# Score banks in a four-unit pattern and paired VectorE transposes in the backward core of a linear-attention plus multi-query-attention kernel

## The chip, the core and the metric

The kernel runs on one core of one Trainium2 chip. The metric is the device time of one execution in microseconds (us): the median of three executions before the change is 1065.62 us (1065.28 to 1067.54). The TensorE clock that was granted over the whole profiled execution is 0.999 of full speed. A unit of time used below is the "block" of eight units of the main loop, explained in the section on the kernel.

## The reference

The reference takes two attention layers, their inputs, weights and the gradient of the joint output, and returns the output and all nine gradients. Layer A is linear attention (feature map phi on q and k, no softmax). Layer B is softmax attention with 16 query heads and one shared key and value head. Cut to layer B, on which the change works:

```python
q = (x @ wq).reshape(B, S, H, Dh).transpose(0, 2, 1, 3)     # S = 2048, H = 16, Dh = 28
k, v = x @ wk, x @ wv                                        # one head for all
scores = jnp.einsum("bhqd,bkd->bhqk", q, k) * (Dh ** -0.5)
o = jnp.einsum("bhqk,bkd->bhqd", softmax(scores), v)
out_B = o.transpose(0, 2, 1, 3).reshape(B, S, H * Dh) @ wo
# returned: out = concat(out_A, out_B) and the vjp of it for x, wq, wk, wv, wo (and A's inputs)
```

For the gradients the kernel needs, per head, e = exp(scale * q k^T - shift) (not normalised), dP = dO v^T, dS = e * dP, and from them o = e v, dq = dS k, dk = dS^T q, dv = e^T dO. Normalisation and the row sums are folded into the small operands (a column of ones in v, the first column of dO).

## The kernel before

**Before the main loop** (up to about 218 us of the span) stand layer A with its gradients and the projections of layer B. **After it** (from about 1017 us) stand the last sums: dwq, dwk, dwv, dx of layer B and their stores.

**The main loop** (`for u in range(NU + 28)`, NU = 512) is a software pipeline written out by hand: inside `tc.manual_schedule()` every engine executes its instructions in the order in which the Python loop issues them. A block b = u // 8 is a pair of heads and 256 queries; unit u of it covers 256 of the 2048 keys for both heads h = 0, 1. Scores, dP and dS are kept transposed, keys on the 128 partitions: a tile 128 x 512 holds two groups of 128 keys by 256 queries. In iteration u the engines do:

- **TensorE**: `rows_SD(u)` makes the scores of unit u (banks `sp[0]`, `sp[1]` of PSUM, one per head) and dP of unit w = u - 16 (banks `DB[0]`, `DB[1]`, one buffer each). A product of 32 rows by 256 columns fills half a bank, so each bank takes two matmuls, and the list `todo` is their order. Then, in even iterations, the transposes `onat_T` (u % 8 = 2) and `don_T` (u % 8 = 6) and the output projection `out_proj` (u % 8 = 0), all three into the bank `spare`; then `o_dq`, which adds two units to o and two to dq (16 matmuls); then `dv_mm` (four matmuls a call, four calls a block). In odd iterations come 16 matmuls of dk (`dk_m`).
- **ScalarE**: exp of the first head's scores (line 924, "exp0"), the copy of `DB[1]` to SBUF (938, "cp"), exp of the second head's scores (970, "exp1"). Nothing else in the steady loop.
- **VectorE**: the product dS = dP * e of the first head, straight from `DB[0]` (936, "the product"); small evictions: `out_proj` (727) at u % 8 = 0, oTs (952) at 1, reciprocal and normalisation (799, 800) at 2, dq (955) at 3, a row sum (812) at 4, doT (828) at 6; and at the end of each iteration the 32 x 32 transpose of dS of unit y = u - 18 (1003, "the transpose", 512 words of two bf16 each), which dk reads.
- **GpSimd**: the product dS of the second head (939), small products, copies of queries, a few stores.
- **SyncE**: every four units one DMA transpose of e (972) into `eN`, which dv reads; four DMA transposes of queries every 64 units.

PSUM: three score banks `SB`, used round robin: iteration u takes `SB[2u % 3]` and `SB[(2u + 1) % 3]`, and the third is `spare`. So what is `spare` in an even iteration is the first score bank of the odd one that follows. Buffers in SBUF: `dsT` (dS) 5, one unit each; `eN` (transposed e) 6, four units each; `dsx` (transposed dS) 2, eight units each. `dsT` buffers are also used for staging outside the loop (`sbuf`).

Engines meet through semaphores, and a waiting instruction holds up what is behind it on its engine.

Of the kernel before, what the change touches and what calls it, by code (L numbers as in the profile page):

```python
# [16 lines left out]
D = 448  # L17
# [8 lines left out]
def kernel(  # L26
# [604 lines left out]
    with ExitStack() as cs_:  # L631
        pe_ = cs_.enter_context(tc.tile_pool(name="ceT", bufs=1, side="right"))
        pn_ = cs_.enter_context(tc.tile_pool(name="ceN", bufs=1, side="right"))
        pd_ = cs_.enter_context(tc.tile_pool(name="cdsT", bufs=5, side="right"))
# [10 lines left out]
        dsT, dsx, qX, don, doT, rl, prod = ({} for _ in range(7))  # L645
        ETs = [pe_.tile([P, 4, 2, 512], BF16, name=f"eT{i}") for i in range(5)]
        ENs = [pn_.tile([P, 32, P], BF16, name=f"eN{i}") for i in range(6)]
# [3 lines left out]

        def eN(b, c):
            return ENs[(2 * b + c // 2) % 6][:, 16 * (c % 2):16 * (c % 2) + 16, :]
# [9 lines left out]
        def rows_SD(u, sp, dp):  # L663
# [4 lines left out]
            if sp is not None and dp is not None and u % 2 == 0:  # L668
                todo = [(0, 0), (0, 1), (1, 0)] * 2 + [(1, 1)] * 2
# [71 lines left out]
        def post_load(k):  # L741
            if k == 4:
                post["dkvT"], mix = (eN(61, c).rearrange("p a b -> p (a b)") for c in range(2))
                post["dkvn"] = mix[:, 0:1024]
# [20 lines left out]
        def gwo(n0, n1):  # L765
            for n in range(n0, n1):
                st, g_ = (n // 2, n % 2) if n < 32 else (n % 16, n // 16)
                if st == 0:
                    post[g_] = SB[g_ % 2]
                al = post[g_]  # L770
                mm(al[:, 0:D], do_nat[:, st, g_ * P:(g_ + 1) * P], post["gb"][st][:, 0:D], start=(st == 0),
                   stop=(st == NS - 1))
                if st == NS - 1:
                    sb = pd_.tile([P, 2, 512], BF16, name="dsT")[:, 0, 0:D]
                    nc.scalar.activation(out=sb, in_=al[:, 0:D], func=ACT.Copy)
                    for j in range(4):
                        h = 4 * g_ + j
                        nc.gpsimd.dma_start(out_8[h * DH:(h + 1) * DH, :], sb[32 * j + 1:32 * j + 1 + DH, :])  # L778
# [116 lines left out]
        with tc.manual_schedule():  # L895
            nc.sync.dma_start(wo, wo_d[:, 0:D].rearrange("(g p) c -> p g c", p=P))
            qX[0] = pqa_.tile([P, 4, 2, 512], BF16, name="qX")
            for g in range(4):
                st = pd_.tile([P, 2, 512], BF16, name="dsT").rearrange("p a (n j) -> p a n j", j=32).rearrange(
# [4 lines left out]
            for u in range(NU + 28):  # L904
# [3 lines left out]
                sp = [SB[(2 * u + h) % 3] for h in range(2)] if hasS else None  # L908
                dp = DB if hasD else None
                spare = SB[(2 * u + 2) % 3] if hasS else SB[2]  # L910
                rows_SD(u, sp, dp)
                if (b := due(u, 10)) is not None:
                    onat_T(b, spare)
# [11 lines left out]
                if u == 1:  # L925
                    q_shift(pn3, shifts[3], [pd_.tile([P, 2, 512], BF16, name="dsT").rearrange("p a b -> p (a b)").bitcast(F32)
                                             for _ in range(1)])
# [4 lines left out]
                if hasD:  # L932
                    dst = pd_.tile([P, 2, 512], BF16, name="dsT")
# [35 lines left out]
                if hasS:  # L969
                    nc.scalar.activation(out=eT(u)[:, 1, :], in_=sp[1][:, :], func=ACT.Exp, scale=scale)  # L970
                    if u % 4 == 3:
                        nc.sync.dma_start_transpose(ENs[u // 4 % 6][:, :, :],
# [9 lines left out]
                else:  # L982
                    o_dq((u - 2, u - 1), (u - 20, u - 19))
                    b, n = divmod(u - 20, 8)
                    for k in {0: (0, 1), 2: (2,), 6: (3,)}.get(n, ()) if 0 <= b < NB else ():
                        dv_mm(dv_acc, b, k // 2, k % 2)
# [12 lines left out]
                if 0 <= y < NU:  # L999
                    b, tp = divmod(y, 8)  # L1000
                    if tp == 0:
                        dsx[b] = px_.tile([P, 8, 2, 2, 256], BF16, name="dsx")
                    nc.vector.transpose(  # L1003
                        out=dsx[b][:, tp, :, :, :].rearrange("p h t c -> p (h t c)").bitcast(F32),
                        in_=dsT[y][:, :, :].rearrange("p h c -> p (h c)").bitcast(F32))
# [11 lines left out]
        def sbuf():  # L1017
            return pd_.tile([P, 2, 512], BF16, name="dsT")[:, 0, :]
# [11 lines left out]
        def dwq(c):  # L1030
# [9 lines left out]
            if c == 3:  # L1040
                odd = pd_.tile([P, 2, 512], BF16, name="dsT").rearrange("p a b -> p (a b)").bitcast(F32)[0:64, 0:D]
# [77 lines left out]
```

## Time and profile before

| what | value |
|---|---|
| median of three executions | 1065.62 us |
| span of the profiled execution, first to last instruction | 1064.7 us |
| busy share of the span: TensorE, VectorE, ScalarE, GpSimd | 96%, 84%, 82%, 73% |
| first exp0 of the main loop starts at | 218.5 us |
| exp0 of unit 511 starts at | 989.0 us |
| last transpose ends about | 1017.6 us |
| mean time of eight units, from unit 24 to unit 504 | 12.11 us |

The profiled execution has a span of 1064.7 us. What lies around it in the measured time is about 0.9 us, if it stands at the median.

How to read the profile: "x512" is a count, then comes the busy time of the group and the mean length of one instruction. In the timeline a row is start, length, engine, line, operation, written tile <- read tiles; neighbours of one group are merged into one row (x2, x16). Both ScalarE and VectorE start an instruction before the end of the one ahead of it is recorded, so lengths overlap: the cost of an instruction on its engine is the distance between starts.

### The profile page before, as it was taken

Reading aid. Unit: us, or ns where it says so; the run is one execution under the profiler, and the core shown is the slowest. Engines: PE = TensorE matmul, PEld = TensorE weight load, DVE = VectorE, ACT = ScalarE, POOL = GpSimd, SP = SyncE. Lnnn points to the kernel's source line nnn. Section 1 sums busy time; section 2 is a strip of 40 time slices with the busy share of each in tenths; the row PEclk is TensorE's granted clock in tenths of the full one; section 3 lists DMA queues with packets and bytes.
Section 4 is the critical chain, followed back from the end, with each engine's and each line's share of the span. In section 5 each row is a group of like instructions: output and inputs, shape, how many; then the busy total and the mean of one; then the engine's idle time right before and its main releaser. Section 6 shows DMA issues by size and latency. Waiting matters only on the chain.

```text
span 1064.7 us, 40036 instructions
## 1 busy us (share of the span) xinstructions
PE 1023.1 (96%) x16241; PEld 489.1 (46%) x16241; DVE 899.5 (84%) x1797; ACT 870.4 (82%) x1741; POOL 780.7 (73%) x1033
## 2 busy tenths in 40 slices
PE   9999999998999999999999999999999999999998
PEld 5555455434444444444444444444444444444444
DVE  7887400459999999999999999999999999999942
ACT  6463222489999999999999999999999999999522
POOL 6001242218888898899889989988998999888881
PEclk9999999999999999999999999999999999999999
DMA  9849899079999999999999999999999999999963
GB/s 264 167 108 192 171 203 246 22 137 181 193 188 196 182 203 189 188 202 191 197 181 197 181 196 195 193 189 194 196 197 192 199 190 183 208 190 177 222 141 89
DMA packets 689937, 195.15 MB, mean 183 GB/s; under 512 B 670616, under 2 KB 687792, under 8 KB 689752
## 3 DMA queue, kind: packets, MB, share of 16 engines
q1 hardware_dynamic: 680152, 179.92, 99.6%
q0 software_dynamic: 4640, 8.71, 2.9%
q10 hardware_dynamic: 4960, 3.96, 1.3%
q8 instruction: 127, 2.08, 0.8%
q14 instruction: 58, 0.48, 0.2%
HBM read 12.60 MB, written 10.84 MB: 22 GB/s over the span
## 4 chain that ended last, share of the span: by engine, by line
PE 43%; ACT 32%; issue 14%; POOL 5%; DVE 4%; DMA 1%; ACTq 0%; DVEq 0%; POOLq 0%
ACT cp L938 16%; PE agen L81 14%; ACT eT L970 13%; PE agen L656 10%; PE aacc L656 10%; PE aacc L81 5%; POOL dsT L939 3%; PE aacc L790 2%; ACT eT L924 2%; PE aacc L821 1%; DVE dsT L936 1%; DVE dsx L1003 1%; DMA out_dram<-dsT 1%; POOL eT L754 1%; POOL out_dram L778 0%
## 5 line engine op out<-in xcount | busy, mean ns | idle before, releaser
L939 POOL TENSOR_TENSOR dsT<-cp,eT 128x512 bf16<-128x512 bf16 x512 | 587.9, 1156 | 78.9 <-ACT cp L938 71.7
L1003 DVE STREAM_TRANSPOSE dsx<-dsT 128x512 f32<-128x512 f32 x512 | 357.6, 699 | 2.9 <-POOL dsT L939 0.8
L656 PEld LDWEIGHTS <-R 32*128 32x128 bf16 (+1 forms) x9104 | 227.9, 94 | 274.1 <-issue 238.4
L936 DVE TENSOR_TENSOR dsT<-agen,eT 128x512 bf16<-128x512 f32 x512 | 341.7, 667 | 10.9 <-PE agen L656 5.6
L938 ACT ACTIVATE cp<-agen 128x512 bf16<-128x512 f32 x512 | 315.8, 617 | 12.3 <-PE agen L656 11.2
L924 ACT ACTIVATE eT<-aacc 128x512 bf16<-128x512 f32 x512 | 313.6, 612 | 14.8 <-PE agen L656 4.8
L970 ACT ACTIVATE eT<-aacc 128x512 bf16<-128x512 f32 x512 | 322.2, 629 | 0.0
L656 PE MATMUL agen<-dsx,qX 32*32 32x512 bf16 x4096 | 267.6, 375 | 0.0
L656 PE MATMUL agen<-doT,R 32*128 32x256 bf16 x2048 | 247.1, 269 | 3.4 <-DVE dsT L936 1.4
L656 PE MATMUL aacc<-R,R 32*128 32x256 bf16 (+1 forms) x2240 | 218.2, 268 | 7.2 <-DVE oTs L800 2.5
L656 PE MATMUL agen<-eT,R 128*32 128x256 bf16 x2048 | 157.5, 274 | 0.1
L656 PE MATMUL agen<-dsT,R 128*32 128x256 bf16 x2048 | 156.8, 274 | 0.1
L656 PEld LDWEIGHTS <-qX 32*32 32x32 bf16 x4096 | 79.8, 89 | 113.7 <-issue 53.3
L656 PE MATMUL aacc<-eN,don 128*32 128x512 bf16 x1024 | 97.1, 379 | 0.1
L81 PEld LDWEIGHTS <-R 128*128 128x128 bf16 (+1 forms) x517 | 40.8, 98 | 43.5 <-issue 11.5
L406 POOL COPY pk<-R 128x256 bf16<-128x256 bf16 x4 | 1.6, 397 | 73.8 <-DVE R L366 73.7
L81 PE MATMUL agen<-R,R 128*128 128x448 bf16 (+1 forms) x180 | 42.1, 361 | 0.6 <-ACT R L225 0.6
L832 POOL COPY qst<-R 128x512 bf16<-128x512 bf16 x56 | 34.2, 611 | 4.0 <-DMA qX<-qst 3.9
L656 PEld LDWEIGHTS <-don 128*32 128x32 bf16 x1024 | 33.8, 97 | 1.4 <-issue 1.0
L804 POOL TENSOR_TENSOR prod<-R,oTs 128x128 f32<-128x128 bf16 x64 | 27.6, 431 | 9.3 <-DVE oTs L800 9.3
L422 DVE TENSOR_TENSOR osb<-aacc,pr 64x448 bf16<-64x448 f32 x2 | 1.2, 618 | 38.3 <-DMA out_dram<-osb 24.4
L955 DVE TENSOR_SCALAR R<-agen 64x256 bf16<-64x256 f32 x64 | 27.3, 427 | 3.6 <-PE agen L656 1.6
(231 smaller groups left out, 967.8 us busy)
## 6 DMA issues: line engine op xcount, KB each, us to landing
out_dram<-osb ACTq DMA_DIRECT2D x22, 112.0 KB
eN<-eT SPq DMA_TRANSPOSE x128
xa<-in_A_x_dram SPq DMA_DIRECT2D x8, 224.0 KB
ga<-in_grad_out_dram SPq DMA_DIRECT2D x4, 448.0 KB
xa<-in_grad_out_dram POOLq DMA_DIRECT2D x4, 448.0 KB, 6.1
out_dram<-wdq POOLq DMA_DIRECT2D x8, 224.0 KB, 4.0
eT<-in_grad_out_dram SPq DMA_DIRECT2D x4, 448.0 KB
eT<-in_B_x_dram SPq DMA_DIRECT2D x4, 448.0 KB
```

The lines of the kernel that those rows point to most:

```text
L81: nc.tensor.matmul(out_ap, lhsT=lhsT, rhs=rhs, start=start, stop=stop, tile_position=(0, 0))
L656: nc.tensor.matmul(out, lhsT=lhsT, rhs=rhs, start=start, stop=stop, tile_position=pos, skip_group_check=True)
L790: nc.tensor.transpose(onp[:, qb, :, :].rearrange("p h c -> p (h c)"), oTs[0:64, qb * P:(qb + 1) * P], identF[0:64, 0:64], tile_position=(0 ...
L804: nc.gpsimd.tensor_tensor(out=prod[b][:], in0=dnv, in1=os_, op=ALU.mult)
L832: eng.tensor_copy(out=st.rearrange("p (b s) a j -> p b s a j", s=2)[:, :, s, :, :], in_=src.unsqueeze(2).to_broadcast([P, 4, 4, 32]))
L924: nc.scalar.activation(out=eT(u)[:, 0, :], in_=sp[0][:, :], func=ACT.Exp, scale=scale)
L936: nc.vector.tensor_tensor(out=dst[:, 0, :], in0=dp[0][:, :], in1=ew[:, 0, :], op=ALU.mult)
L938: nc.scalar.activation(out=cp[:, :], in_=dp[1][:, :], func=ACT.Copy)
L939: nc.gpsimd.tensor_tensor(out=dst[:, 1, :], in0=cp[:, :], in1=ew[:, 1, :], op=ALU.mult)
L955: nc.vector.tensor_scalar(out=qT_B[g][64 * hp:64 * hp + 64, qc * 256:(qc + 1) * 256], in0=oq[64:128, 0:256], scalar1=scale, scalar2=None, ...
L970: nc.scalar.activation(out=eT(u)[:, 1, :], in_=sp[1][:, :], func=ACT.Exp, scale=scale)
L1003: nc.vector.transpose(out=dsx[b][:, tp, :, :, :].rearrange("p h t c -> p (h t c)").bitcast(F32), in_=dsT[y][:, :, :].rearrange("p h c -> p ...
```

## The change

Four things are changed in the main loop, and two buffer sets are sized anew.

1. **Score banks.** The round robin over three banks is replaced by a pattern over four units: (first head, second head, spare) = (0, 1, 2), (0, 2, 1), (1, 0, 2), (1, 2, 0) for u % 4 = 0 to 3. In even iterations the spare bank is always bank 2, and it is the second head's bank of the odd iteration that follows; the first head of an odd iteration takes the same bank as the first head of the even one before.
2. **Order of the matmuls.** In odd iterations `todo` becomes first heads first: scores h0, dP h0, scores h0, dP h0, then scores h1, dP h1, scores h1, dP h1. Half of `o_dq` (o of unit u - 2, dq of unit u - 20) is issued directly after `rows_SD`, ahead of the transposes and of `out_proj`; the other half stays behind them.
3. **Transposes of dS.** dS of two units lies in one buffer (4 buffers of two units instead of 5 of one). One transpose of 1024 words at the end of each odd iteration replaces two of 512 words.
4. **dv.** The four calls of `dv_mm` of block b move from units 20, 20, 22, 26 to 18, 20, 20, 22 behind the block's first unit, and `eN` has 5 buffers instead of 6.

Staging tiles outside the loop now come from `half()`, which hands out the halves of a two-unit `dsT` buffer.

```diff
-        pd_ = cs_.enter_context(tc.tile_pool(name="cdsT", bufs=5, side="right"))
+        pd_ = cs_.enter_context(tc.tile_pool(name="cdsT", bufs=4, side="right"))
...
-        ENs = [pn_.tile([P, 32, P], BF16, name=f"eN{i}") for i in range(6)]
+        ENs = [pn_.tile([P, 32, P], BF16, name=f"eN{i}") for i in range(5)]
...
+        halves = []
+
+        def half():
+            if not halves:
+                t = pd_.tile([P, 2, 2, 512], BF16, name="dsT")
+                halves.extend([t[:, 0, :, :], t[:, 1, :, :]])
+            return halves.pop(0)
...
-            return ENs[(2 * b + c // 2) % 6][:, 16 * (c % 2):16 * (c % 2) + 16, :]
+            return ENs[(2 * b + c // 2) % 5][:, 16 * (c % 2):16 * (c % 2) + 16, :]
...
-            if sp is not None and dp is not None and u % 2 == 0:
-                todo = [(0, 0), (0, 1), (1, 0)] * 2 + [(1, 1)] * 2
+            if sp is not None and dp is not None:
+                todo = [(0, 0), (1, 0)] * 2 + [(0, 1), (1, 1)] * 2 if u % 2 else \
+                    [(0, 0), (0, 1), (1, 0)] * 2 + [(1, 1)] * 2
...
-                sp = [SB[(2 * u + h) % 3] for h in range(2)] if hasS else None
+                b0, b1, spare = ((SB[i] for i in ((0, 1, 2), (0, 2, 1), (1, 0, 2), (1, 2, 0))[u % 4]) if hasS else SB)
+                sp = [b0, b1] if hasS else None
                 dp = DB if hasD else None
-                spare = SB[(2 * u + 2) % 3] if hasS else SB[2]
                 rows_SD(u, sp, dp)
+                if u % 2 == 0:
+                    o_dq((u - 2,), (u - 20,))
...
-                    dst = pd_.tile([P, 2, 512], BF16, name="dsT")
+                    if w % 2 == 0:
+                        pairs[w // 2] = pd_.tile([P, 2, 2, 512], BF16, name="dsT")
+                    dst = pairs[w // 2][:, w % 2, :, :]
...
-                        nc.sync.dma_start_transpose(ENs[u // 4 % 6][:, :, :],
+                        nc.sync.dma_start_transpose(ENs[u // 4 % 5][:, :, :],
...
-                    o_dq((u - 2, u - 1), (u - 20, u - 19))
-                    b, n = divmod(u - 20, 8)
-                    for k in {0: (0, 1), 2: (2,), 6: (3,)}.get(n, ()) if 0 <= b < NB else ():
+                    o_dq((u - 1,), (u - 19,))
+                    b, n = divmod(u - 18, 8)
+                    for k in {0: (0,), 2: (1, 2), 4: (3,)}.get(n, ()) if 0 <= b < NB else ():
                         dv_mm(dv_acc, b, k // 2, k % 2)
...
-                if 0 <= y < NU:
+                if 0 <= y < NU and y % 2:
                     b, tp = divmod(y, 8)
-                    if tp == 0:
+                    if tp == 1:
                         dsx[b] = px_.tile([P, 8, 2, 2, 256], BF16, name="dsx")
                     nc.vector.transpose(
-                        out=dsx[b][:, tp, :, :, :].rearrange("p h t c -> p (h t c)").bitcast(F32),
-                        in_=dsT[y][:, :, :].rearrange("p h c -> p (h c)").bitcast(F32))
+                        out=dsx[b][:, tp - 1:tp + 1, :, :, :].rearrange("p u h t c -> p (u h t c)").bitcast(F32),
+                        in_=pairs[y // 2].rearrange("p u h c -> p (u h c)").bitcast(F32))
...
         def sbuf():
-            return pd_.tile([P, 2, 512], BF16, name="dsT")[:, 0, :]
+            return half()[:, 0, :]
```

More of the change, by code (lines that the diff above doesn't have):

```diff
@@ L643 @@
         oq, dk_acc = (psA.tile([P, 512], F32, name="agen") for _ in range(2))
-        dsT, dsx, qX, don, doT, rl, prod = ({} for _ in range(7))
+        dsT, dsx, qX, don, doT, rl, prod, pairs = ({} for _ in range(8))
         ETs = [pe_.tile([P, 4, 2, 512], BF16, name=f"eT{i}") for i in range(5)]
-        ENs = [pn_.tile([P, 32, P], BF16, name=f"eN{i}") for i in range(6)]
+        ENs = [pn_.tile([P, 32, P], BF16, name=f"eN{i}") for i in range(5)]
         def eT(u):
             return ETs[u // 4 % 5][:, u % 4, :, :]
+        halves = []
[4 more added lines that the diff above has]
+            return halves.pop(0)
         def eN(b, c):
-            return ENs[(2 * b + c // 2) % 6][:, 16 * (c % 2):16 * (c % 2) + 16, :]
+            return ENs[(2 * b + c // 2) % 5][:, 16 * (c % 2):16 * (c % 2) + 16, :]
         def mmt(out, lhsT, rhs, pos, start, stop):
@@ L742, in post_load @@
             if k == 4:
-                post["dkvT"], mix = (eN(61, c).rearrange("p a b -> p (a b)") for c in range(2))
+                post["dkvT"], mix = (eN(61, c).rearrange("p a b -> p (a b)") for c in (2, 3))
                 post["dkvn"] = mix[:, 0:1024]
@@ L773, in gwo @@
                 if st == NS - 1:
-                    sb = pd_.tile([P, 2, 512], BF16, name="dsT")[:, 0, 0:D]
+                    sb = half()[:, 0, 0:D]
                     nc.scalar.activation(out=sb, in_=al[:, 0:D], func=ACT.Copy)
@@ L898 @@
             for g in range(4):
-                st = pd_.tile([P, 2, 512], BF16, name="dsT").rearrange("p a (n j) -> p a n j", j=32).rearrange(
+                st = half().rearrange("p a (n j) -> p a n j", j=32).rearrange(
                     "p a (n b) j -> p (a n) b j", b=4)
@@ L925 @@
                 if u == 1:
-                    q_shift(pn3, shifts[3], [pd_.tile([P, 2, 512], BF16, name="dsT").rearrange("p a b -> p (a b)").bitcast(F32)
-                                             for _ in range(1)])
+                    q_shift(pn3, shifts[3], [half().rearrange("p a b -> p (a b)").bitcast(F32)])
+                    halves.clear()
                     dv_acc = psA.tile([P, 512], F32, name="aacc")
@@ L1040, in dwq @@
             if c == 3:
-                odd = pd_.tile([P, 2, 512], BF16, name="dsT").rearrange("p a b -> p (a b)").bitcast(F32)[0:64, 0:D]
+                odd = half().rearrange("p a b -> p (a b)").bitcast(F32)[0:64, 0:D]
                 nc.scalar.activation(out=odd, in_=al[64:128, 0:D], func=ACT.Copy)
```

## The prediction

> **What bounds the kernel now.** I looked first at the busy time by engine in a stretch of the main loop, then at the groups of VectorE in it, then at the timeline of single units, and last at the chain of work behind the loop. The stretch from 300 to 940 us (columns: length, then PE, weight loads, DVE, ACT, POOL busy with counts, clock, DMA share, GB/s):
>
> ```profile
> 300.00:940.00 640.00, 618.08 (x12141) 290.49 (x12138) 625.68 (x1216) 633.31 (x1274) 579.12 (x698) 1.00 1.19 193
> ```
>
> Three engines look full. Lengths overlap, however, so I go by distances between starts. ScalarE around an odd unit (559.54 starts exp0 of a unit with u % 8 = 3):
>
> ```profile
> 557.86 0.63 ACT L924 ACTIVATE eT<-aacc 128x512 bf16<-128x512 f32 x1
> 558.33 0.64 ACT L938 ACTIVATE cp<-agen 128x512 bf16<-128x512 f32 x1
> 558.81 0.66 ACT L970 ACTIVATE eT<-aacc 128x512 bf16<-128x512 f32 x1
> 559.54 0.60 ACT L924 ACTIVATE eT<-aacc 128x512 bf16<-128x512 f32 x1
> 560.03 0.59 ACT L938 ACTIVATE cp<-agen 128x512 bf16<-128x512 f32 x1
> ```
>
> The reader should see a step of 0.48 us from instruction to instruction, and 0.73 from exp1 of the even unit to exp0 of the odd one. Eight units at 24 x 0.48 are 11.5 us; they take 12.11 on average (11.97 to 12.02 in quiet blocks). The 0.6 us are lost before odd exp0s alone (means 0.57, 0.76, 0.59, 0.57 in place of 0.48), which wait for VectorE: the small eviction of the spare bank, or the product itself. So the bound is a round trip between VectorE and TensorE, with ScalarE close behind. VectorE in the same stretch (mean ns of one in the middle):
>
> ```profile
> L1003 DVE STREAM_TRANSPOSE dsx<-dsT 128x512 f32<-128x512 f32 x425 | 296.9, 699 | 2.0 <-POOL dsT L939 0.2
> L936 DVE TENSOR_TENSOR dsT<-agen,eT 128x512 bf16<-128x512 f32 x424 | 283.1, 668 | 6.1 <-PE agen L656 1.5
> L955 DVE TENSOR_SCALAR R<-agen 64x256 bf16<-64x256 f32 x53 | 22.6, 427 | 1.7
> L952 DVE COPY oTs<-agen 64x256 f32<-64x256 f32 x53 | 21.5, 405 | 0.0
> ```
>
> ```profile
> 559.62 0.66 DVE L936 TENSOR_TENSOR dsT<-agen,eT 128x512 bf16<-128x512 f32 x1
> 560.30 0.43 DVE L955 TENSOR_SCALAR R<-agen 64x256 bf16<-64x256 f32 x1
> 560.76 0.71 DVE L1003 STREAM_TRANSPOSE dsx<-dsT 128x512 f32<-128x512 f32 x1
> 561.50 0.69 DVE L936 TENSOR_TENSOR dsT<-agen,eT 128x512 bf16<-128x512 f32 x1
> 562.11 0.27 DVE L812 TENSOR_REDUCE Dq<-prod 128x4 f32<-128x128 f32 x1
> 562.31 0.70 DVE L1003 STREAM_TRANSPOSE dsx<-dsT 128x512 f32<-128x512 f32 x1
> 562.93 0.65 DVE L936 TENSOR_TENSOR dsT<-agen,eT 128x512 bf16<-128x512 f32 x1
> ```
>
> Between any two products stands a transpose of about 0.62 us. That matters because `DB[0]` is one buffer: dP of the next unit can be made only when the product has read the bank, and the next product needs that dP. The round trip stands here (a merged row gives the span of its group):
>
> ```profile
> 422.99 0.69 DVE L936 TENSOR_TENSOR dsT<-agen,eT 128x512 bf16<-128x512 f32 x1
> 423.59 0.70 DVE L1003 STREAM_TRANSPOSE dsx<-dsT 128x512 f32<-128x512 f32 x1
> 423.73 0.26 PE L656 MATMUL agen<-doT,R 32*128 32x256 bf16 x1
> 424.19 0.36 PE L656 MATMUL agen<-doT,R 32*128 32x256 bf16 x2
> 424.54 0.69 DVE L936 TENSOR_TENSOR dsT<-agen,eT 128x512 bf16<-128x512 f32 x1 [0.24 <-PE agen L656]
> ```
>
> The product ends at 423.68; the first dP matmul starts 0.05 later; the second head-0 matmul starts at 424.19, is done 0.28 later (424.46), and the next product starts 0.07 after that. Where nothing comes between the two matmuls they start 0.11 apart. (Here a matmul of the other head, waiting for cp until 424.17, came between; the new odd order removes that.)
>
> **The change part by part.**
>
> *Transposes.* 512 instructions become 256 of twice the length. No row shows 1024 words. From 128 words (812: 0.275 us) to 256 (952: 0.405) a word costs 1.02 ns, from there to 512 (936: 0.65) 0.96 ns, so 512 more words add 0.49 to 0.52 to the 0.62 between starts: 1.11 to 1.14. Two old ones, 1.24, are the upper bound. I take 1.14, nearest to the longer rows with a margin for rounding; 0.10 saved a pair, 0.4 us a block, if VectorE were the only limit. But the order is now product(even), small work, product(odd), small work, transpose, product(even). The cover of the round trip from even to odd product goes. Start to start it costs the product 0.65 + 0.05 + 0.11 + 0.27 + 0.07 = 1.15 us. VectorE itself would need 0.58 to 0.61 plus small work of 0.2 (u % 8 = 0, 4, 6) or 0.4 (u % 8 = 2), so it idles 0.35, 0.15, 0.35, 0.35. From odd to even the transpose covers the trip with room.
>
> [...]
>
> *The sum for a block.* Four times even to odd, 1.15: 4.60. Odd product to what follows: 0.61 after an idle engine, three times, and 0.69 before line 955: 2.52. Lines 952 and 955 to the transpose: 0.33 + 0.35 = 0.68. Four transposes, 1.14: 4.56. Together 12.36 us, against 11.97 to 12.02 in quiet blocks and 12.11 on average. The average holds disturbances (GpSimd behind by query copies, so that cp waits for its buffers); with ScalarE idling 0.85 a block some are absorbed. So 0.25 to 0.36 a block; I take 0.30. From unit 24 to 511 there are 61 blocks: +18 us. Bounds: with 1.11 for a transpose, and 1.14 for the trip, a block takes 12.19: +5 us. With 1.24 and nothing absorbed, 12.76 + 0.1: +46; I count that end as far, since it denies any fixed part.
>
> *Banks, order, o_dq.* The odd exp0 no longer waits for the eviction after the even product: its second scores matmul follows the first dP matmul, so exp0 starts 0.05 + 0.28 + 0.03 = 0.36 after the even product's end; the row at u % 8 = 4, without an eviction, shows 0.40. That alone would free up to 0.6 us a block, but what is late next is the even product, held by the pair's order. The eviction now gates exp1 and the head-1 matmuls of the odd unit, 0.95 later on ScalarE; it ends at most 1.06 after the even product's start, before exp1 needs it. The eight matmuls of the first half of `o_dq` (0.22 us) go ahead of `onat_T`, `don_T` and `out_proj`, where TensorE waited 21 us in the stretch for exp1; that wait is covered. Is TensorE in time? From the start of one even product, by the trace's starts: 0.70 to the odd dP, 0.42 for the odd scores and dP, dk 0.96, even scores and dP 0.31, change of tile shape 0.20, two halves of `o_dq` 0.44, change back 0.30: 3.33, and the spare work and dv on top (0.19; 0.26 + 0.22; 0.43; 0.11 + 0.22 for u % 8 = 0, 2, 4, 6): 3.5 to 3.8. It is wanted after the pair's period, 2.9 to 3.3, plus 0.7. So it is in time, or up to 0.05 late behind u % 8 = 6: at most 0.05 x 61 = 3 us.
>
> *dv and `eN`.* Counts and queues are unchanged, SyncE's order too. The transposed e lands at least 7.8 us before dv reads it; two units sooner (3 us) leaves 4.8. The buffer's next DMA is issued one unit after its last reader, as before, where at least 2 us lay between. If that cover went, each late landing would hold TensorE by its own lateness, and none is. Cost: nothing.
>
> *Outside the loop.* The two ends of the pipeline (16 units each with only one half of the work) I leave at +/- 2 us. Behind the loop the staging buffers turn from 5 into 8 halves, released in pairs:
>
> ```profile
> 1051.19 3.81 DMA out_dram<-dsT
> 1055.00 0.04 DVEq L1061
> ```
>
> VectorE waits here 3.9 us for a store before it may write a dx tile. With eight halves the first two dx tiles find a free buffer and the third still waits for that store; TensorE gets two tiles of 0.76 us further ahead: -1.5 us (0 to -3.8).
>
> Sum: 1065.6 + 18 - 1.5, rounded up for TensorE's lateness: **1083 us**. The profiled span, 1064.7, plus about 0.9 around it stands at the median, so nothing is added for the execution.
>
> **The rivals.**
>
> *The round trip doesn't bind, and the kernel gets faster.* For it: VectorE's own work falls to 10.9 us a block, and exp0 loses its wait for evictions. It decides if the step from even to odd product falls below 1.08 us, since 4 x 0.07 is the margin between 12.36 and 12.11. Against: each term of 1.15 is at or next to its recorded minimum. At ScalarE's 11.5 us a block it would be 61 x 0.6 = 37 us less, 1029; halfway, 1047.
>
> *Savings and exposed idle cancel.* The lower bounds above, with the full gain behind the loop: 1065.6 + 5 - 3.8 = 1067, within 0.2% (2 us, about what a measurement of this kernel can tell from no change) with a little luck.
>
> *TensorE binds as well.* If head-1 matmuls of odd units wait for evictions (u % 8 = 0, 2, 6) and push dk, scores and exp0 of the next even unit by 0.1 to 0.35, the block grows by some 0.3 more: 61 x 0.6 = 37, 1101 us. For it: TensorE has 0.1 to 0.2 us to spare a pair. Against: waiting is mostly in pairs that VectorE stretches by lines 952 and 955 anyway.
>
> **How the numbers follow.** Round trip binds, about 1083 (1068 to 1098): 0.70. TensorE too, 1101: 0.10. Cancelled, 1067: 0.06, of which most is within 0.2%. Faster, 1029 to 1060: 0.14. The range leaves out the faster case and the far half of TensorE's: 1064 to 1102. Faster 0.14, same 0.04, slower 0.82.
>
> **What would show it.** In the changed profile: the transpose at 1.2 us a piece, 256 times; products with an idle time of 0.3 us before every odd one, released by TensorE's `agen`; even to odd starts 1.15 apart; exp0 of odd units idle before it for about 0.9 us a block in all; eight units in 12.3 to 12.5 us; dx's wait behind the loop shorter. I am wrong if odd products follow even ones by less than 1.08, if a 1024-word transpose takes less than 1.1, or if the chain of waits in the loop names dv, `eN` or GpSimd.

## The result and the profile after

| | before | after |
|---|---|---|
| median, us | 1065.45 (1064.49 to 1067.54) | 1096.2 (1095.93 to 1097.84) |
| span of the profiled execution, us | 1064.7 | 1094.2 |
| first exp0 of the loop to exp0 of unit 511, us | 770.5 | 800.3 |
| of it the first four blocks, us | 45.8 | 48.7 |
| mean block after these (units 32 to 504), us | 12.10 | 12.56 |
| exp0 of unit 511 to the end of the span, us | 75.8 | 75.8 |

The change makes the kernel slower by a factor of 1.028, 95% interval [1.0264, 1.0295]: 30.7 us. All of it lies in the main loop: 59 blocks at 0.46 us more are 27 us, the first four blocks add 2.9, and behind the loop nothing changes. (By the two spans the loss is 29.5 us. Here and in every other run with both numbers the measured time is 1.7 us above the span, so the profiled execution of the kernel before stood near 1066.4 us and not at the median.)

In after.py the lines of before stand a little lower: exp0 is 935 (924 before), the product 949 (936), cp 951 (938), exp1 983 (970), the transpose 1016 (1003), the evictions oTs 965 (952) and dq 968 (955), the row sum 821 (812), doT 837 (828), normalisation 808 and 809 (799, 800), the matmul helper 664 (656).

The stretch from 300 to 940 us of the changed kernel (length, then PE, weight loads, DVE, ACT, POOL busy with counts, clock, DMA share, GB/s):

```profile
300.00:940.00 640.00, 623.87 (x11663) 264.66 (x11666) 590.64 (x965) 620.90 (x1224) 560.09 (x673) 1.00 1.11 185
```

VectorE has fewer instructions (965 in place of 1216) and is busy 35 us less, ScalarE 12 us less; the clock stays at 1.00. Less work got done in the same stretch: 408 units instead of 424. VectorE's groups there (busy, mean ns of one, then idle before and what ended it):

```profile
L949 DVE TENSOR_TENSOR dsT<-agen,eT 128x512 bf16<-128x512 f32 x408 | 275.7, 676 | 44.6 <-PE agen L664 35.4
L1016 DVE STREAM_TRANSPOSE dsx<-dsT 128x1024 f32<-128x1024 f32 x204 | 251.5, 1233 | 0.8
L968 DVE TENSOR_SCALAR R<-agen 64x256 bf16<-64x256 f32 x51 | 21.7, 426 | 1.6
L965 DVE COPY oTs<-agen 64x256 f32<-64x256 f32 x51 | 20.6, 405 | 0.0
```

The new thing is the idle time before the product: 44.6 us, 35.4 of it put down to TensorE's `agen`, where before had 6.1 and 1.5. The product waits for dP. One such wait on all engines (merged rows give the span of their group; rows of other work are left out):

```profile
524.76 0.69 DVE L949 TENSOR_TENSOR dsT<-agen,eT 128x512 bf16<-128x512 f32 x1
...
525.37 0.28 DVE L821 TENSOR_REDUCE Dq<-prod 128x4 f32<-128x128 f32 x1
525.50 0.26 PE L664 MATMUL agen<-doT,R 32*128 32x256 bf16 x1 [0.37 <-DVE dsT L949]
...
525.64 0.27 PE L664 MATMUL agen<-doT,R 32*128 32x256 bf16 x1
...
525.91 0.69 DVE L949 TENSOR_TENSOR dsT<-agen,eT 128x512 bf16<-128x512 f32 x1 [0.27 <-PE agen L664]
```

The even product ends at 525.45; the first dP matmul of the odd unit starts 0.05 later, having waited 0.37 us for exactly that; the second starts at 525.64, ends at 525.91, and the odd product follows at once. From product to product: 1.15 us, while VectorE has only the row sum to do in between. Now VectorE over a whole run of units:

```profile
521.12 0.64 DVE L949 TENSOR_TENSOR dsT<-agen,eT 128x512 bf16<-128x512 f32 x1
521.70 0.15 DVE L808 RECIPROCAL rl<-aacc 128x4 f32<-128x4 f32 x1
521.89 0.29 DVE L809 TENSOR_TENSOR oTs<-aacc,rl 128x128 f32<-128x128 f32 x1
522.30 0.69 DVE L949 TENSOR_TENSOR dsT<-agen,eT 128x512 bf16<-128x512 f32 x1
523.02 0.43 DVE L968 TENSOR_SCALAR R<-agen 64x256 bf16<-64x256 f32 x1
523.48 1.25 DVE L1016 STREAM_TRANSPOSE dsx<-dsT 128x1024 f32<-128x1024 f32 x1
524.76 0.69 DVE L949 TENSOR_TENSOR dsT<-agen,eT 128x512 bf16<-128x512 f32 x1
...
526.52 1.24 DVE L1016 STREAM_TRANSPOSE dsx<-dsT 128x1024 f32<-128x1024 f32 x1
527.68 0.65 DVE L949 TENSOR_TENSOR dsT<-agen,eT 128x512 bf16<-128x512 f32 x1
```

Two things are to be seen. Even to odd takes 1.18 (521.12 to 522.30) and 1.15 (524.76 to 525.91, above). Odd to even takes 1.77 where only the transpose stands between (525.91 to 527.68), and 2.46 across line 968 (522.30 to 524.76). The two kinds follow each other without slack, and a block is their sum. ScalarE, meanwhile, waits:

```profile
524.45 0.59 ACT L951 ACTIVATE cp<-agen 128x512 bf16<-128x512 f32 x1
524.93 0.60 ACT L983 ACTIVATE eT<-aacc 128x512 bf16<-128x512 f32 x1
525.82 0.60 ACT L935 ACTIVATE eT<-aacc 128x512 bf16<-128x512 f32 x1 [0.29 <-PE aacc L664]
526.32 0.59 ACT L951 ACTIVATE cp<-agen 128x512 bf16<-128x512 f32 x1
```

0.89 us from exp1 of the even unit to exp0 of the odd one in place of 0.48: the odd scores stand in TensorE's queue right behind the dP matmul that waits for the product. The chain that ended last says the same for the whole span (by engine, then by line); before it read PE 43%, ACT 32%, DVE 4%:

```profile
PE 74%; DVE 19%; ACT 3%; issue 2%; POOL 1%; DMA 1%; DVEq 0%; ACTq 0%
PE agen L664 34%; PE aacc L664 15%; PE agen L81 14%; DVE dsT L949 8%; DVE dsx L1016 8%; PE aacc L81 7%; DVE R L968 2%; PE aacc L799 1%; ACT cp L951 1%; POOL dsT L952 1%; ACT eT L983 1%; ACT eT L935 1%; DMA dsx<-R 1%; PE aacc L85 0%; PE aacc L830 0%
```

ScalarE has all but left the chain; product, transpose and the matmuls between two products have taken its place.

Behind the loop the wait of 3.9 us for a store's buffer is gone, as the eight staging halves promised, and the time is the same all the same. The dx tiles of VectorE, after:

```profile
1083.29 0.62 DVE L1074 CAST dsT<-agen 128x448 bf16<-128x448 f32 x1 [1.88 <-PE agen L81]
1084.81 0.62 DVE L1074 CAST dsT<-agen 128x448 bf16<-128x448 f32 x1 [0.89 <-PE agen L81]
```

They now wait for TensorE, and each next tile 1.5 us apart is TensorE's pace (two tiles of 0.76, one for ScalarE). Before:

```profile
1055.17 1.28 DVE L1061 CAST dsT<-agen 128x448 bf16<-128x448 f32 x2 [3.92 <-DMA out_dram<-dsT]
1056.86 0.62 DVE L1061 CAST dsT<-agen 128x448 bf16<-128x448 f32 x1 [0.41 <-ACT dsT L1063]
1058.37 0.62 DVE L1061 CAST dsT<-agen 128x448 bf16<-128x448 f32 x1 [0.89 <-ACT dsT L1063]
```

The tile that waited for the store was written together with its successor at once and the row of tiles went on at the same 1.5 us: the wait was covered by TensorE's work.

### The profile page after: what moved, and what is told of

Same layout as the page of the kernel before. It is cut to its first block, busy times and chain, and to the rows that moved or that the text cites. A ratio compares the mean times of both kernels' runs of the same rounds, so it can differ in the third digit from the quotient of the medians.

```text
span 1094.2 us, 38903 instructions
## 1 busy us (share of the span) xinstructions
PE 1057.8 (97%) x16241; PEld 470.6 (43%) x16241; DVE 886.1 (81%) x1541; ACT 885.0 (81%) x1741; POOL 784.3 (72%) x1033
## 3 DMA queue, kind: packets, MB, share of 16 engines
q8 instruction: 127, 2.08, 0.7%
## 4 chain that ended last, share of the span: by engine, by line
PE 74%; DVE 19%; ACT 3%; issue 2%; POOL 1%; DMA 1%; DVEq 0%; ACTq 0%
PE agen L664 34%; PE aacc L664 15%; PE agen L81 14%; DVE dsT L949 8%; DVE dsx L1016 8%; PE aacc L81 7%; DVE R L968 2%; PE aacc L799 1%; ACT cp L951 1%; POOL dsT L952 1%; ACT eT L983 1%; ACT eT L935 1%; DMA dsx<-R 1%; PE aacc L85 0%; PE aacc L830 0%
## 5 line engine op out<-in xcount | busy, mean ns | idle before, releaser
L949 DVE TENSOR_TENSOR dsT<-agen,eT 128x512 bf16<-128x512 f32 x512 | 346.0, 676 | 57.2 <-PE agen L664 45.7
L664 PEld LDWEIGHTS <-R 32*128 32x128 bf16 (+1 forms) x9104 | 211.4, 94 | 353.9 <-issue 331.1
L951 ACT ACTIVATE cp<-agen 128x512 bf16<-128x512 f32 x512 | 315.4, 616 | 13.0 <-PE agen L664 12.3
L1016 DVE STREAM_TRANSPOSE dsx<-dsT 128x1024 f32<-128x1024 f32 x256 | 315.5, 1233 | 1.0
L664 PE MATMUL aacc<-R,R 32*128 32x256 bf16 (+1 forms) x2240 | 298.4, 268 | 4.1 <-ACT eT L935 0.8
L664 PE MATMUL agen<-doT,R 32*128 32x256 bf16 x2048 | 272.2, 270 | 22.9 <-DVE dsT L949 21.8
L664 PE MATMUL agen<-eT,R 128*32 128x256 bf16 x2048 | 181.5, 276 | 0.1
L664 PE MATMUL agen<-dsT,R 128*32 128x256 bf16 x2048 | 181.1, 276 | 0.0
```

The lines of the kernel that those rows point to most:

```text
L664: nc.tensor.matmul(out, lhsT=lhsT, rhs=rhs, start=start, stop=stop, tile_position=pos, skip_group_check=True)
L949: nc.vector.tensor_tensor(out=dst[:, 0, :], in0=dp[0][:, :], in1=ew[:, 0, :], op=ALU.mult)
L951: nc.scalar.activation(out=cp[:, :], in_=dp[1][:, :], func=ACT.Copy)
L1016: nc.vector.transpose(out=dsx[b][:, tp - 1:tp + 1, :, :, :].rearrange("p u h t c -> p (u h t c)").bitcast(F32), in_=pairs[y // 2].rearrang ...
```

## The experiments

All were timed against the kernel before on the same chip; the runs come from several chips, so between runs the ratios compare better than the times. Diffs are against the changed kernel unless said otherwise. The theory: **the transpose used to be the cover of the round trip through the one buffer `DB[0]`; moved behind the odd product it leaves the even-to-odd round trip bare, and the pair of products becomes the bound.** The rivals: TensorE is short of time; the new banks and the new matmul order cost something; dv sooner with one `eN` less costs something; the long instruction does.

**1. Single transposes, all else as changed (e1).**

```diff
-                if 0 <= y < NU and y % 2:
+                if 0 <= y < NU:
...
-                        out=dsx[b][:, tp - 1:tp + 1, :, :, :].rearrange("p u h t c -> p (u h t c)").bitcast(F32),
-                        in_=pairs[y // 2].rearrange("p u h c -> p (u h c)").bitcast(F32))
+                        out=dsx[b][:, tp, :, :, :].rearrange("p h t c -> p (h t c)").bitcast(F32),
+                        in_=pairs[y // 2][:, y % 2, :, :].rearrange("p h c -> p (h c)").bitcast(F32))
```

> The changed kernel with one transpose per unit again (512 words, at the end of each iteration, from the two-unit buffers); banks, order of matmuls and dv as in the change. Theory (the pairing lays the VectorE-TensorE round trip bare between the even and the odd product): a transpose covers it again, and since odd exp0s no longer wait for evictions, eight units take 11.6 to 12.0 us instead of 12.59: 1035 to 1058 us. Rival (the new banks and order of matmuls cost the time, the pairing is harmless or a help): 1095 us or more, eight units 12.5 to 12.9.

Measured: 1066.84 us, ratio to before 0.9994 [0.9984, 1.0003]; blocks of 12.02 and 12.04. VectorE in the same stretch:

```profile
L1016 DVE STREAM_TRANSPOSE dsx<-dsT 128x512 f32<-128x512 f32 x425 | 295.7, 696 | 1.8 <-DVE R L736 0.2
L949 DVE TENSOR_TENSOR dsT<-agen,eT 128x512 bf16<-128x512 f32 x425 | 280.6, 660 | 7.1 <-PE agen L664 4.3
```

The product's wait falls from 44.6 us to 7.1. The whole loss belongs to the paired transpose. But the gain that I expected of the banks and the order without pairing isn't there either: by the code the odd exp0 no longer waits for the eviction, but ahead of odd exp0s ScalarE still loses 0.37 us a block (0.58 in the kernel before), ahead of even ones 0.15 (none before), and eight units still take 12.03 us. VectorE has next to nothing left to give: all the idle time of its groups in the stretch is 16.5 us, 0.3 us a block (14.5 in the kernel before, 49.7 in the changed one). Its steps from product to product, from u % 8 = 0 on, are 1.56, 1.52, 1.70, 1.76, 1.43, 1.19, 1.75, 1.23 us in one kind of block and 1.38, 1.52, 1.70, 1.88, 1.43, 1.19, 1.39, 1.42 in the next (medians). Runs 6 and 9 come back to this.

**2. Pairing alone (e2):** the round robin of the banks, the old order of the odd matmuls and `o_dq` in one piece come back; the paired transpose, dv and the buffers stay as changed.

```diff
-            if sp is not None and dp is not None:
-                todo = [(0, 0), (1, 0)] * 2 + [(0, 1), (1, 1)] * 2 if u % 2 else \
-                    [(0, 0), (0, 1), (1, 0)] * 2 + [(1, 1)] * 2
+            if sp is not None and dp is not None and u % 2 == 0:
+                todo = [(0, 0), (0, 1), (1, 0)] * 2 + [(1, 1)] * 2
...
-                b0, b1, spare = ((SB[i] for i in ((0, 1, 2), (0, 2, 1), (1, 0, 2), (1, 2, 0))[u % 4]) if hasS else SB)
+                sp = [SB[(2 * u + h) % 3] for h in range(2)] if hasS else None
...
-                if u % 2 == 0:
-                    o_dq((u - 2,), (u - 20,))
...
-                    o_dq((u - 1,), (u - 19,))
+                    o_dq((u - 2, u - 1), (u - 20, u - 19))
```

> The changed kernel with the old round robin of score banks, the old order of matmuls and o_dq in one piece; pairing and earlier dv stay. Theory: the round trip is laid bare and, in addition, the odd scores wait for the eviction after the even product, and dP of the odd unit behind them; from even to odd product 1.3 to 1.5 us: 1105 to 1140 us. Rival (banks and order cost the time): back to 1060 to 1070 us.

Measured: 1155.79 us, ratio 1.0819 [1.0802, 1.0837], slower than expected; blocks of 13.5 us. The product waits nearly twice as long as in the changed kernel:

```profile
L946 DVE TENSOR_TENSOR dsT<-agen,eT 128x512 bf16<-128x512 f32 x380 | 256.6, 675 | 86.5 <-PE agen L664 85.0
```

Even to odd takes 1.34, 1.57, 1.16 us at u % 8 = 0, 2, 4, and 1.35 and 1.48 in turn at 6 (changed kernel: 1.12, 1.14, 1.16, 1.12). The three long ones are those with a small eviction of the spare bank behind the even product; u % 8 = 4 has none. By the code, the odd unit's first scores wait with the old banks for that eviction, and its dP stands behind them in TensorE's queue. So banks and order don't cost: they save 57 us by the ratios (60 by the times), but only of a loss that pairing makes. The four corners (ratio to the kernel before in brackets):

| us | single transposes | paired transposes |
|---|---|---|
| old banks and order | 1065.3 (0.9988, run 5 below) | 1155.8 (1.0819) |
| new banks and order | 1066.8 (0.9994) | 1096.2 (1.0280) |

**3 and 4. Is TensorE short of time, or is it the bank?** Run e3 leaves dv's matmuls out (their output isn't computed), which takes 16 matmuls of 512 columns from every block. Run e4 leaves them out too and uses dv's bank as a second `DB[0]` for odd units; nothing else differs.

```diff
-                        dv_mm(dv_acc, b, k // 2, k % 2)
+                        pass
```
```diff
-                dp = DB if hasD else None                                             # e4 only
+                dp = [dv_acc if w % 2 else DB[0], DB[1]] if hasD else None
```

> The changed kernel without the matmuls of dv (dv is left out of the sums; its bank is written once). Takes 0.86 us of TensorE work out of eight units. Theory (bound by the round trip): nearly unchanged, 1088 to 1096 us, eight units 12.45 to 12.6. Rival (TensorE's own work binds): up to 0.86 x 61 = 52 us less, 1044 us.

> As the run without dv, and the bank that dv leaves free takes the first head's dP of odd units, so that dP of the odd unit need not wait for the even product. Pairing, banks and order stay. Theory: the idle time before odd products goes, from even to odd product 0.8 to 1.0 us; eight units fall to ScalarE's 11.5 to 11.8: 1030 to 1048 us, some 45 to 60 less than without dv alone. Rival (the long transposes, banks or order cost the time): as without dv alone, within 5 us.

Measured: e3 1102.12 us, ratio 1.0317 [1.0301, 1.0333]: no faster with TensorE relieved. Its blocks are 12.45 and 12.59 (12.51 and 12.59 in the changed kernel), and the product still waits 43.0 us in the stretch; one last block of 18.65 us adds 6 us and takes it over the expected range. The trace shows what holds that block: VectorE's copies of dv's sums (line 1036, behind the loop in the code) have no dv to wait for, so they run inside it, and the first waits 3.56 us there for a DMA transpose into `eN`. e4: 1061.82 us, ratio 0.9946 [0.9930, 0.9963], 40 us less than e3, 34 of them apart from that last block. The product in e4, odd units (`aacc`) and even ones (`agen`):

```profile
L951 DVE TENSOR_TENSOR dsT<-aacc,eT 128x512 bf16<-128x512 f32 x213 | 146.7, 689 | 12.9 <-PE aacc L664 10.8
L951 DVE TENSOR_TENSOR dsT<-agen,eT 128x512 bf16<-128x512 f32 x214 | 143.3, 670 | 1.8
```

and the unit that waited in the changed kernel:

```profile
524.73 0.69 DVE L951 TENSOR_TENSOR dsT<-agen,eT 128x512 bf16<-128x512 f32 x1
525.33 0.28 DVE L821 TENSOR_REDUCE Dq<-prod 128x4 f32<-128x128 f32 x1
525.53 0.68 DVE L951 TENSOR_TENSOR dsT<-aacc,eT 128x512 bf16<-128x512 f32 x1
```

0.80 us in place of 1.15. The idle time falls from 43.0 to 14.7 us with one more buffer of the bank: the round trip is shown to be the wait. TensorE's load is excluded. e4 was expected faster still; it stops at blocks of 12.0, where the even-to-odd steps are still 1.19 us at u % 8 = 0, 1.02 at 2, and 0.83 and 1.01 in turn at 6, and the step across line 968 (970 here) is still 2.33 and 2.46 in turn. What holds the step at u % 8 = 0 stays open. For a kernel with dv that bank isn't free.

**5. The rest of the change without pairing, banks or order (e5):** the kernel before with dv sooner, five `eN` and the `dsT` buffers of two units.

> The kernel before with the earlier dv, five buffers of transposed e and two-unit buffers of dS alone: old banks, old order, one transpose per unit. If dv and its buffers cost nothing: 1064 to 1069 us, eight units 12.0. If a landing or a buffer were late: 1075 us or more, with dv or the DMA in the waits of the loop. Together with the run that has the pairing alone it gives the price of pairing under the old banks.

Measured: 1065.31 us, ratio 0.9988 [0.9975, 1.0001]. These parts cost nothing.

**6. Single transposes without dv (e6):** the edits of runs 1 and 3 together.

> The changed kernel with one transpose per unit (it ran like the kernel before, eight units in 12.03 us) and without the matmuls of dv (dv left out of the sums). Theory A (with a transpose between any two products VectorE's own queue sets the pace): unchanged, 1060 to 1068 us. Theory B (TensorE's queue sets it: dk, scores, o and dq without a gap): 0.5 to 0.86 us less in eight units, 1014 to 1036 us.

Measured: 1071.55 us, ratio 1.0048 [1.0034, 1.0063]; blocks of 12.02 and 12.04 to the digit as in run 1, and a last one of 18.94 us as in e3, from the same wait, which takes the time over the expected range. TensorE was busy 22 us less in the stretch (610.65 us against 632.70). So the 12.03 us of single transposes aren't TensorE's load.

**7. Place or length (e9)?** Two transposes of 512 words, both at the end of the odd iteration: the changed kernel's place, the old length.

```diff
-                    nc.vector.transpose(
-                        out=dsx[b][:, tp - 1:tp + 1, :, :, :].rearrange("p u h t c -> p (u h t c)").bitcast(F32),
-                        in_=pairs[y // 2].rearrange("p u h c -> p (u h c)").bitcast(F32))
+                    for s in range(2):
+                        nc.vector.transpose(
+                            out=dsx[b][:, tp - 1 + s, :, :, :].rearrange("p h t c -> p (h t c)").bitcast(F32),
+                            in_=pairs[y // 2][:, s, :, :].rearrange("p h c -> p (h c)").bitcast(F32))
```

> The changed kernel, but in place of the one transpose of 1024 words at the end of each odd iteration two of 512 words stand there, one behind the other; all else is as in the change. Theory (it is the place of the transposes that lays the round trip bare, not their length): as slow as the change and slower by the saving of the long form, 2 x 0.62 - 1.16 = 0.08 us a pair, 0.3 us in eight units: 12.9 us, 1110 to 1122 us. Rival (the long instruction itself costs the time): back to 1064 to 1072 us.

Measured: 1109.55 us, ratio 1.0401 [1.0386, 1.0417], 13 us slower than the changed kernel (just under the expected range).

```profile
523.24 1.29 DVE L1017 STREAM_TRANSPOSE dsx<-dsT 128x512 f32<-128x512 f32 x2
524.46 0.65 DVE L949 TENSOR_TENSOR dsT<-agen,eT 128x512 bf16<-128x512 f32 x1
525.03 0.26 DVE L736 CAST ot<-aacc 128x112 bf16<-128x112 f32 x1
525.57 0.69 DVE L949 TENSOR_TENSOR dsT<-agen,eT 128x512 bf16<-128x512 f32 x1 [0.28 <-PE agen L664]
```

Two short ones take 1.22 us to the next product where the long one takes 1.16: the long form saves 0.06 a pair, 4 x 0.06 x 61 = 15 us. The place alone costs 4.0%, the form gives 1.2 back. What decided is the place: VectorE was nearly full without pairing (16.5 us idle in the stretch, run 1), and the loss comes whatever the length.

**8. The step across line 968 (e7, e8, e13).** In the changed kernel this step is 0.2 us longer than the parts I had added up. Looked at by blocks, it has two lengths in turn. A block whose pair of heads has an even number:

```profile
434.47 0.69 DVE L949 TENSOR_TENSOR dsT<-agen,eT 128x512 bf16<-128x512 f32 x1
435.20 0.43 DVE L968 TENSOR_SCALAR R<-agen 64x256 bf16<-64x256 f32 x1
435.55 1.23 DVE L1016 STREAM_TRANSPOSE dsx<-dsT 128x1024 f32<-128x1024 f32 x1
436.81 0.69 DVE L949 TENSOR_TENSOR dsT<-agen,eT 128x512 bf16<-128x512 f32 x1
```

and the next one, of an odd number:

```profile
446.99 0.69 DVE L949 TENSOR_TENSOR dsT<-agen,eT 128x512 bf16<-128x512 f32 x1
447.71 0.43 DVE L968 TENSOR_SCALAR R<-agen 64x256 bf16<-64x256 f32 x1
448.17 1.25 DVE L1016 STREAM_TRANSPOSE dsx<-dsT 128x1024 f32<-128x1024 f32 x1
449.45 0.69 DVE L949 TENSOR_TENSOR dsT<-agen,eT 128x512 bf16<-128x512 f32 x1
```

Elsewhere in the loop an instruction of VectorE that waits for nothing starts 0.07 to 0.08 us before the recorded end of the one ahead. Here line 968 starts 0.03 after it, and so does the product behind the transpose; the transpose starts 0.08 before the end of 968 in the one kind of block and 0.03 after it in the other. Each lost overlap is 0.11 us: 2.34 us with two of them, 2.46 with three, 2.11 by the parts without any. Is it the form of 968 (a multiplication by a constant), the instruction as a whole, or what stands ahead of it? In e7 it is a plain copy (the factor is applied to a small operand ahead of the loop); e8 is the same with single transposes. In e13 the eviction, the two removed lines below, is left out with nothing in its place, and dq's part of the output isn't computed.

```diff
-                    nc.vector.tensor_scalar(out=qT_B[g][64 * hp:64 * hp + 64, qc * 256:(qc + 1) * 256],
-                                            in0=oq[64:128, 0:256], scalar1=scale, scalar2=None, op0=ALU.mult)
+                    nc.vector.tensor_copy(out=qT_B[g][64 * hp:64 * hp + 64, qc * 256:(qc + 1) * 256],   # e7, e8
+                                          in_=oq[64:128, 0:256])
```

> The changed kernel with line 968 as a plain copy; the factor is folded into the keys that dq is made with, so all sums are kept. In the change the step from the odd product at u % 8 = 3 to the next even one takes 2.34 to 2.39 us, at u % 8 = 1, with a plain copy, 2.10. If the scaled form of the instruction makes the difference, 0.24 to 0.29 us in eight units go: 1076 to 1082 us. If it is the place (the destination, the wait behind it), no change: 1094 to 1098.

> One transpose per unit and line 968 as a plain copy, all sums kept. If VectorE's queue sets the pace of eight units (12.03 us) and the scaled instruction costs it 0.2 us there, 11.8 us and 1050 to 1056 us, faster than both kernels. If TensorE's queue sets it, or the scaled form costs nothing: 1062 to 1068 us.

> The changed kernel with the eviction of line 968 left out (dq's part of the output is not computed), pairing and all else as changed. The step from odd product at u % 8 = 3 to the next product is 2.39 us with the eviction, 1.77 at u % 8 = 5 and 7 where nothing but the transpose stands there. Theory: the eviction and the overlap lost beside it belong together, and the step falls to 1.75 to 1.8: eight units 11.95 to 12.0 us in place of 12.59, 61 x 0.61 = 37 us less, 1057 to 1062 us. First rival: the lost overlap comes from the instruction before (the normalisation of line 809 at u % 8 = 2, which waits for a result of VectorE's own) and stays: step 1.85 to 1.95, 1063 to 1069 us. Second rival: the round trip is not what sets the blocks there, and other steps grow by what this one loses: 1090 to 1097 us.

Measured: e7 1098.02 us, ratio 1.0286 [1.0271, 1.0301], blocks of 12.51 and 12.59 as changed; e8 1066.36 us, ratio 0.9994 [0.9985, 1.0004]: not the form. e13 1068.38 us, ratio 1.0013 [1.0001, 1.0026]. Its step at u % 8 = 3:

```profile
526.33 0.69 DVE L949 TENSOR_TENSOR dsT<-agen,eT 128x512 bf16<-128x512 f32 x1
526.94 1.23 DVE L1012 STREAM_TRANSPOSE dsx<-dsT 128x1024 f32<-128x1024 f32 x1
528.10 0.65 DVE L949 TENSOR_TENSOR dsT<-agen,eT 128x512 bf16<-128x512 f32 x1
```

1.77 us, the value of u % 8 = 5 and 7, with all overlaps back: the eviction and the lost overlap belong together, and the instruction before it is excluded. In time 6 us of what was expected are missing, since the next step, at u % 8 = 4, grew from 1.16 to 1.26. (The time falls into the range of the first rival, but that rival stood on a step of 1.85 to 1.95.)

What line 968 does unlike its neighbours is to read partitions 64 to 127 and to write partitions 0 to 63 or 64 to 127, by the number of its pair of heads; line 965 is as large, reads and writes from partition 0, and keeps its overlap (519.64 + 0.41 against 519.97 in the timeline). One other line of the loop changes its partitions, and it is a test of this by itself: the copy doT (837) reads and writes partitions 0 to 63 in one block and 64 to 127 in the next, and differs in nothing else but which of its two buffers it writes. From partition 0:

```profile
527.68 0.65 DVE L949 TENSOR_TENSOR dsT<-agen,eT 128x512 bf16<-128x512 f32 x1
528.25 0.27 DVE L837 COPY doT<-aacc 64x256 bf16<-64x256 bf16 x1
```

and from partition 64:

```profile
540.13 0.65 DVE L949 TENSOR_TENSOR dsT<-agen,eT 128x512 bf16<-128x512 f32 x1
540.82 0.29 DVE L837 COPY doT<-aacc 64x256 bf16<-64x256 bf16 x1
```

It starts 0.07 to 0.08 before the end of the product in the first and 0.03 after it in the second, and so in every block between 260 and 1000 us (29 and 30 of them). Line 968, which reads from partition 64 in every block, starts 0.03 after the end of the product in all 58 there. What stands behind it goes with the partition that it wrote from: the transpose starts 0.08 before the end of 968 where that wrote from partition 0 (29 blocks), and 0.03 after it where it wrote from partition 64 (29); the product behind the transpose starts 0.03 after its end in both. That is two and three lost overlaps in turn, as in the two fences. The kernel before has the same rows: line 955 starts 0.03 after the product in 61 of 61 blocks, the transpose behind it 0.08 before the end of 955 in 30 and 0.03 after it in 31, the next product 0.03 after the transpose in all. That the start partition is the cause is a reading of these two lines; why an instruction loses its overlap there, no run shows.

**9. What holds 12.03 us without pairing (e10, e12)?** e10 is run 1 with the normalisation (809), and GpSimd's work behind it, moved behind the transpose of u % 8 = 2, so that the transpose starts sooner. e12 is run 1 without line 968 (dq's part of the output isn't computed).

```diff
             nc.vector.reciprocal(out=r_[:], in_=onp[:, :, :, 0:1])
+            late[b] = (onp, r_, os_)
+
+        def o_norm2(b):                              # called behind the transpose
+            onp, r_, os_ = late.pop(b)
             nc.vector.tensor_tensor(out=os_, in0=onp[:, :, :, :], in1=r_[:].to_broadcast([P, 2, 2, 32]), op=ALU.mult)
...
```

> New banks and order, one transpose per unit, and the normalisation (multiply after the reciprocal, with what follows from it) moved behind the transpose of its unit, u % 8 = 2; all sums kept. VectorE's multiply there waits for VectorE's own reciprocal just ahead, and the instructions behind it start 0.03 us after, not 0.08 before, the end of the one ahead. If that wait breaks the overlap: 0.1 to 0.3 us less in eight units, 1048 to 1061 us, faster than both kernels. If not, or if the later eviction holds the odd scores: 1064 us or more.

> The changed kernel with one 512-word transpose per unit (as in the run with single transposes), and the eviction of line 968 (dq of a block, 64x256, once in eight units) left out, so that dq's part of the output is not computed. Theory: without pairing VectorE's own queue sets the 12.03 us of eight units; the step from product to product across line 968 falls from 1.82 us to the 1.2 to 1.35 of a step with nothing between but a transpose, and eight units to 11.5 to 11.6 us (24 x 0.48 us on ScalarE is then the floor): 61 x 0.5 = 30 us less than the 1066.8 of single transposes, 1031 to 1045 us. Rival: another loop (TensorE's order, cp and GpSimd) keeps 12.0 us of its own; then other steps grow by what this one loses, and the time is 1064 to 1068 us.

Measured: e10 1083.92 us, ratio 1.0157 [1.0135, 1.0180]: the spare bank comes free later, the odd unit's second-head matmuls stand behind it, cp follows exp0 of u % 8 = 3 by 0.75 us in place of 0.49, and blocks take 12.2 to 12.5 us. The step across line 968 got no shorter (1.90 us, and 968 still starts 0.03 after the end of the product), so the reciprocal's wait wasn't what broke the overlap. The eviction of the spare bank, then, can't go later than it is. e12 1060.02 us, ratio 0.9931 [0.9904, 0.9958]: between the two expectations. The step across 968 fell from 1.76 and 1.88 in turn to 1.28, as the first theory had it, but the step at u % 8 = 5 grew from 1.19 to 1.41, and undisturbed blocks went from 12.03 to 11.85 only. From exp0 of u % 8 = 4 to unit 6 ScalarE there runs at its 0.48 us a step without a gap: in that half of the block it is the next bound. Some blocks of 12.2 to 13.6 us, in which GpSimd waits for the query DMAs (13.2 us in the stretch; 2.6 in run 1), give half of that or more back. So VectorE's queue sets the pace without pairing, but the others have only some 0.2 us a block to spare.

None of these versions that compute everything beats the kernel before by more than its measurement can tell (best: e5, 0.9988 [0.9975, 1.0001]).

## Why the prediction was right, and where it was off

Forecast were 1083 us and slower; measured are 1096.2, inside the range and 13 us above the number. By the prediction's own steps:

- *Even to odd, 1.15 us four times, 4.60.* Right: 1.12, 1.14, 1.16, 1.12 by units, 4.53 in sum. The terms are in the fence (0.05 to dP, 0.14 to its second half, 0.27 to the product). e4 shows that the bank is the cause.
- *A 1024-word transpose, 1.14.* 1.158 between starts where nothing disturbs it, 0.02 more: the plain odd-to-even steps are 1.77, 1.77 and 2.10 in place of 1.75, 1.75 and 2.08.
- *Line 955 (now 968) to the next product, 0.69 + 0.35 + 1.14 = 2.18 us.* **This term was mis-sized:** 2.34 and 2.46 in turn, 2.40 on average. Of the 0.22, the way from the product to 968 has 0.03 (0.72), from 968 to the transpose 0.05 (0.35 and 0.46 in turn; I had read the shorter one), and from the transpose to the product 0.13 (1.27): that product loses its overlap as well. The rows for both stood in the prediction's own timeline, where line 955 takes 0.46 to the transpose (560.30 to 560.76) and that transpose 0.74 to the next product (560.76 to 561.50) against 0.62 elsewhere, and I took the shorter ones.
- *The block, 12.36; growth of 0.30.* 12.55, and growth of 0.46. The 0.19 of the block are the two points above (0.26) less the 0.07 gained on even to odd. That disturbances are absorbed (0.05 of 0.11 was allowed for) went further: 12.56 on average against 12.55 undisturbed.
- *Ends of the pipeline, +/- 2 us.* +2.9 in the first four blocks. They take 48 to 50 us in every paired kernel here and 46 to 47 in every single one, whatever the banks: pairing costs there as well.
- *Behind the loop, -1.5 (0 to -3.8).* 0, the end at which nothing is gained: the wait disappeared as foreseen, but TensorE's pace had covered it.
- *The kernel before is bound by a round trip, and VectorE's own work falls to 10.9 us a block.* Not so: VectorE idles 0.27 us a block in the kernel before (14.5 us in the stretch), and with the new banks and order its queue still takes 12.03 (run 1); in the changed kernel it idles 49.7 us in the stretch, which leaves some 11.6 of 12.56 us a block. No run shows the 10.9. A sum of short steps leaves out the lost overlaps of run 8. The forecast itself didn't rest on this sum; the faster rival did.
- *dv and `eN`, nothing.* Right (e5). *TensorE at most 0.05 late.* Right (e3); the rival in which it binds has no support.
- *What would show it:* the transposes (1.23 us, 256 times), and 1.15 from even to odd are as written; the wait of about 0.3 us before odd products, released by `agen`, is 0.27 at u % 8 = 0 and 4, and less at 2 and 6. Blocks of 12.3 to 12.5 were forecast and are 12.5 and 12.6. ScalarE idles 1.05 us a block, forecast 0.9, but only 0.46 of it before odd exp0s; 0.48 come before even ones, behind the long step.

Of the rivals, the faster one was to be decided by an even-to-odd step under 1.08, which none of the four is. Its other assumption, that the banks' gain would come through if nothing else bound, falls with run 1: VectorE's queue holds 12.03 us by itself.

## What to carry to other kernels

An instruction that stands between two users of a single-buffered bank may be that bank's cover: ask what runs during the round trip before moving it, and price the bare trip (here 0.05 + 0.14 + 0.27 and the product itself, 1.15 us) against what merging instructions saves (0.06 us a pair). A second buffer of the bank took most of that cost away here (idle time from 43.0 to 14.7 us, e4), though it gained next to nothing over the kernel before (ratio 0.9946); without one, the place cost 4.0% and the merge gave 1.2 back (e9). And take a step's price from the row with the same neighbours: in the kernel before the same transpose took 0.62 us to the next product, and 0.74 with line 955 just ahead.

## What the runs showed of the hardware

- Two transposes of 512 words merged into one saved 0.06 us (1.22 between starts in e9, 1.16 in the changed kernel).
- Line 968, an eviction that reads partitions 64 to 127 between instructions that start at partition 0, came with two or three lost overlaps of 0.11 us, on itself and on what follows, up to two instructions later: 2.34 or 2.46 us in place of 2.11 by the parts. With its arithmetic replaced by a copy (e7) blocks stayed at 12.51 and 12.59 us. The copy 837 lost its overlap in the 30 blocks from partition 64 (it starts 0.03 after the end of the product) and kept it in the 29 from partition 0 (0.07 to 0.08 before).
- The wait of 3.9 us for a store behind the loop went without any effect on the time (75.8 us from exp0 of unit 511 to the end, before and after): TensorE's tiles for VectorE, 1.5 us apart, set the pace there.
